# A conditioned transformer block in split float16 on one core: early transfers, GpSimd's tiles, scale inverses and held GELU steps put in another order

## The chip, the core and the metric

The chip is a Trainium2. The kernel runs on one of its cores, which has a matrix engine (TensorE, PE in the profile), a vector engine (VectorE, DVE), an engine for functions of single elements (ScalarE, ACT), a general engine (GpSimd, POOL) and an engine that only issues transfers here (SyncE, SP). Each engine takes its instructions in the order in which they were written down. They wait for one another by semaphores. The metric is the time of one execution on the device, in microseconds (us).

## The reference

A block of width 512 works on 2048 rows. Six modulation rows come from a condition vector. Attention has 32 query heads, 8 key and value heads and a window of the last 512 keys. The feed-forward part has an inner width of 1792 and a GELU gate.

```python
mod = silu(c) @ w_mod                       # sa, ca, ga, sb, cb, gb: six rows of 512
h = layernorm(x) * (1 + ca) + sa
q = (h @ wq)                                # 2048 rows, 32 heads of 128
k, v = k_cache[..., -512:, :], v_cache[..., -512:, :]   # 8 heads, each used by 4 query heads
p = softmax(q @ k.T * 128 ** -0.5)
x = x + ga * ((p @ v) @ wo)
h = layernorm(x) * (1 + cb) + sb
x = x + gb * ((gelu(h @ w_gate) * (h @ w_up)) @ w_down)  # gelu in its tanh form
```

All inputs and the output are float32.

## The kernel before

**Products.** Each product of two float32 matrices is three float16 matmuls: both operands are split into a high half, which is the rounded value, and a low half, which is the remainder, and high x high, low x high and high x low are added up (`mm3`, lines L86, L87 and L88). A half pair is made in one of two ways. `split_post` (L631 to L633) takes the high half on ScalarE and the low half on VectorE; it is used for queries (`qt`) and for attention outputs (`ot`). `halves` (L148 to L153) does both on GpSimd; it is used for weights, keys and values, after a multiplication by their scale (`times`, L156). The probabilities `p` are split in `high` (ScalarE, L883) and `low` (VectorE, L888).

**Scales.** So that float16 holds the values, each tile of weights, keys or values is multiplied by a scale that comes from its sum of squares. ScalarE sums the squares by partition (L212), TensorE adds over the partitions (`sums`, L216, the bank `pst`), VectorE copies the sum out (L177, L179 or L227), GpSimd raises it to the power one half and multiplies it on (L229, L233), and VectorE takes the reciprocal (`kinv` L244, `lr` L259, `wsc` L267, `osc` L280, `dsc` L303, `vsc` L606). The reciprocal is not written down at once: `then` (L235) puts it into the list of a later slot, two slots on. GpSimd's weight steps that use the scale come after it.

**Slots.** Attention is 512 slots. A slot t handles one tile of 128 query rows of one head: TensorE's scores `ps`, VectorE's maximum (L862), ScalarE's exponential (L871). In the same slot the probabilities of slot t - 2 get their high half and those of slot t - 3 their low half. `low` also issues the transfer that transposes `p` into `pt` (a DMA transpose on SP's queue), from which TensorE later forms `po`, probabilities times values. Between these steps TensorE takes three pieces of other work from a list: query products `pq`, `po`, and the output products `py`, which read the tiles `wo`. After that the slot runs its lists: plain steps (stores among them), the loads ("l") and the tile steps ("w"). What `then` and `split_post` put off runs in the list "d", ahead of the exponential.

**Groups.** 16 slots form a group, which starts at slot t0 = 16 g and uses one pair of query heads with its weight tiles `w`. There are two halves of 16 groups, one for each half of the rows. In the first half the tiles are made; most are stored (`kept`) and read back in the second half. The tiles of groups 1 and 2 are made by `plain_steps`. From group 3 on the weights are combined to sums and differences for a product with seven terms (`set_steps`, steps s0 to s4; their places before t0 stand in `SETPOS`, for group 3 in `SETPOS2`).

**Where the work is put.** A helper `sched` gets a list of slots for the steps of one tile. It puts the load some three slots ahead of the first step, as far as a free buffer allows (five buffers `raw`, two buffers `rw`). Other things are put at a slot by hand with `at`: the stores of the first keys and values, the loads and steps of the differences of input blocks (`sched_combos`; `CB` is their base slot), and the steps of `wo`. The four tiles of `wo` for a pair of groups are read twice: `WOS` lists the slots for the sums of squares and `WOP` those in which GpSimd multiplies them by `gs` (gate row times scale, L551) and splits them. One row of these tables is for the first pair of groups, one for the second, and so on; a fourth row of `WOP` serves the pairs 6 and 7. `k_items` and `v_items` do the same for keys and values. All transfers are issued on SP's one queue in the order written down, each waiting there until its buffer is free.

**The feed-forward part.** In the second half of attention, `prep_set` (weights of gate and up) and `prep_wd` (weights of down) make its tiles in the same manner. After slot 512 its products run. The first gate results are held back: `result` is put into the list `hold`, and in slot T + 2 = 514 the held tiles are worked off one after the other. Each goes through four steps: ScalarE squares (L1149), VectorE adds and multiplies, ScalarE takes tanh, VectorE multiplies (L1153). ScalarE's copy `fg<-fa` (L772) empties a bank that TensorE needs for its next product.

Of the kernel before, what the change touches and what calls it, by code (L numbers as in the profile page):

```python
# [17 lines left out]
P = 128  # L18
# [45 lines left out]
def block_kernel(ctx: ExitStack, tc: tile.TileContext, x, kT, v, wq, wo, wg, wu, wd, cT, wc, wm, out):  # L64
# [170 lines left out]
    def then(fn):  # L235

        if now[0] < 0:
            fn()
        else:
            at(("d", now[0] + 2), fn)  # L240

    def k_spread(g, m, go=True, ps=None):
        norm2(col("kmax", g), m, 1, 1.0, ps)
        inv = lambda: nc.vector.reciprocal(col("kinv", g), col("kmax", g))  # L244
        return then(inv) if go else inv
# [6 lines left out]
    def w_spread(pr, m, w=None):  # L252
# [13 lines left out]
        if now[0] >= 0:  # L266
            then(lambda: (nc.vector.reciprocal(col("wsc", pr), w), inv(), last()))  # L267
# [324 lines left out]
    def v_items(g):  # L592
# [7 lines left out]
        def spread():  # L600
# [5 lines left out]
            then(lambda: nc.vector.reciprocal(col("vsc", g), w))  # L606
# [408 lines left out]
    at(7, lambda: store(("k", 0), KV[0, 0, 0]))  # L1015
    at(9, lambda: store(("v", 0), KV[0, 0, 1]))
# [66 lines left out]
    for g in range(NG):  # L1083
# [54 lines left out]
    def f_items(q, hold=None):  # L1138
# [6 lines left out]

        def result(key, src):
            if m == 0:
                sq = pool.tile([P, QB], F32, tag="v16", name="sq", bufs=2)
                nc.scalar.activation(sq, src, AF.Square, scale=col("finv", f_scale(q)))  # L1149
                nc.vector.scalar_tensor_tensor(sq, sq, 1.0 / GELU_A, src, op0=ALU.add, op1=ALU.mult)  # L1150
                nc.scalar.activation(sq, sq, AF.Tanh, scale=col("tsc", f_scale(q)))
                dst = tmp("fg") if key == "21" else src
                nc.vector.scalar_tensor_tensor(dst, sq, 1.0, src, op0=ALU.add, op1=ALU.mult)  # L1153
                G[n, key] = dst
# [51 lines left out]
    def prep_set(q, b):  # L1206
# [24 lines left out]
        def s2():  # L1231
# [5 lines left out]
        sched(b, (lambda: set_load(key, srcs, 0), [lambda: pair_stat(key, m, 0), nop]), b + 8, kind="rw")  # L1237
        sched(b + 1, (lambda: set_load(key, srcs, 1), [lambda: pair_stat(key, m, 1), lambda: f_spread(f_scale(q), m["m"]), s2, nop]),
              b + 4, b + 8, b + 9, kind="rw")
        sched(b + 6, (outs[0][1], [s0, keep_it(0)]), b + 9)  # L1240
        sched(b + 7, (outs[3][1], [s1, keep_it(3)]), b + 10)
        sched(b + 8, (outs[1][1], [lambda: made(1, RAW[key][0]), keep_it(1)]), b + 11)
        sched(b + 9, (outs[2][1], [lambda: made(2, RAW[key][1]), keep_it(2)]), b + 12)
# [250 lines left out]
```

## Time and profile before

| what | value |
| --- | --- |
| time, median of 3 runs | 1792.94 us (1790.93 to 1799.85) |
| profiled execution, its own time | 1795.36 us |
| its span in the profile | 1793.1 us |
| TensorE busy | 1739.8 us, 97% |
| VectorE busy | 1446.9 us, 81% |
| ScalarE busy | 1210.5 us, 68% |
| GpSimd busy | 873.6 us, 49% |
| transfers | 330.76 MB, 184 GB/s on the mean |

The profile shows one execution. A row of a group gives line, engine, operation, output and inputs with partitions x elements, the count, busy time and the mean time of one in ns. A row of a timeline gives the start in us, the duration, the engine, the line and the tiles; in square brackets behind it is the time for which the engine stood idle before, and what ended that wait. A row of a table by stretches begins with the stretch in us; it then gives, in order, its length with TensorE's busy time, and the busy times of weight loads, VectorE, ScalarE and GpSimd with their numbers of instructions, then the granted TensorE clock as a share of full speed, the mean busy share of the 16 DMA engines and GB/s. A row of a transfer gives the issuing queue, the count and the median us from issue to landing.

### The profile page before, as it was taken

How to read it: one execution, taken by the hardware profiler on the slowest of the kernel's cores; microseconds unless marked ns; L12 is line 12 of the kernel's file. 1: busy time of each engine (PE TensorE's matmuls, PEld its weight loads, DVE VectorE, ACT ScalarE, POOL GpSimd, SP SyncE). 2: the span in 40 equal slices, each digit the busy share in tenths (PEclk: the TensorE clock that was granted, in tenths of full speed). 3: DMA queues.
4: the chain of work that ended last, by engine and by line, in shares of the span. 5: the costliest groups of instructions: out<-in, count | busy, mean ns of one | idle time of the engine just before them, and what ended most of it. 6: DMA issues, size and time to landing. Idle time of an engine off the chain costs nothing.

```text
span 1793.1 us, 26035 instructions
## 1 busy us (share of the span) xinstructions
PE 1739.8 (97%) x8094; PEld 795.6 (44%) x8094; DVE 1446.9 (81%) x2518; ACT 1210.5 (68%) x2811; POOL 873.6 (49%) x1100
## 2 busy tenths in 40 slices
PE   7989999999999999999999999999998999999999
PEld 4434444444444444444444444444443444444443
DVE  7778889888888888888888888888885758676676
ACT  5867787887877777677778787777774355344342
POOL 4689768686787873236475565555520024000000
PEclk9989999999999999999999999999999999999999
DMA  6989798999999888999999999999885633252221
GB/s 223 214 180 225 180 218 206 235 200 227 214 211 211 194 189 164 228 214 238 200 206 202 233 217 202 212 214 203 197 191 137 213 124 112 74 176 86 86 68 56
DMA packets 663850, 330.76 MB, mean 184 GB/s; under 512 B 553248, under 2 KB 576032, under 8 KB 663712
## 3 DMA queue, kind: packets, MB, share of 16 engines
q1 hardware_dynamic: 663424, 328.58, 78.5%
q8 instruction: 64, 1.05, 0.2%
q14 instruction: 74, 0.61, 0.1%
q10 hardware_dynamic: 288, 0.52, 0.1%
HBM read 134.88 MB, written 59.90 MB: 109 GB/s over the span
## 4 chain that ended last, share of the span: by engine, by line
PE 62%; DVE 13%; POOL 9%; ACT 7%; issue 5%; DMA 4%; SPq 0%; POOLq 0%; ACTq 0%; DVEq 0%
PE py L86 6%; PE py L87 6%; PE py L88 6%; PE ps L86 4%; PE ps L88 4%; PE ps L87 4%; PE po L86 3%; PE po L88 3%; PE po L87 3%; DVE p L888 3%; DVE nm L862 3%; PE fa L86 2%; PE fa L88 2%; PE fa L87 2%; ACT ee L871 2%
## 5 line engine op out<-in xcount | busy, mean ns | idle before, releaser
L871 ACT ACTIVATE ee<-ps,nm 128x512 f32<-128x512 f32 x512 | 350.9, 685 | 265.9 <-DVE nm L862 252.5
L888 DVE SCALAR_TENSOR_TENSOR p<-ee,rr,p 128x512 f16<-128x512 f32 x512 | 466.1, 910 | 0.0
L862 DVE TENSOR_REDUCE nm<-ps 128x1 f32<-128x512 f32 x512 | 349.2, 682 | 80.5 <-PE ps L88 78.6
L883 ACT ACTIVATE p<-ee,rr 128x512 f16<-128x512 f32 x512 | 365.2, 713 | 5.8 <-DMA pt<-p 5.2
L86 PE MATMUL ps<-k,qt 128*128 128x512 f16 x512 | 195.2, 381 | 18.2 <-DVE qt L633 12.4
L86 PE MATMUL po<-pt,v 128*128 128x512 f16 x512 | 195.3, 381 | 5.0 <-DMA pt<-p 2.4
L86 PE MATMUL py<-wo,ot 128*128 128x512 f16 x512 | 194.5, 380 | 1.8 <-DVE ot L633 1.8
L88 PE MATMUL po<-pt,v 128*128 128x512 f16 x512 | 195.3, 381 | 0.0
L87 PE MATMUL po<-pt,v 128*128 128x512 f16 x512 | 195.2, 381 | 0.0
L87 PE MATMUL ps<-k,qt 128*128 128x512 f16 x512 | 195.0, 381 | 0.0
L88 PE MATMUL ps<-k,qt 128*128 128x512 f16 x512 | 194.9, 381 | 0.0
L87 PE MATMUL py<-wo,ot 128*128 128x512 f16 x512 | 194.4, 380 | 0.0
L88 PE MATMUL py<-wo,ot 128*128 128x512 f16 x512 | 194.3, 379 | 0.0
L879 DVE RECIPROCAL rr<-rr 128x2 f32<-128x2 f32 x256 | 41.5, 162 | 98.7 <-ACT rr L876 96.6
L362 POOL TENSOR_TENSOR rs<-rs,nhalf 128x1 f32<-128x1 f32 x32 | 19.2, 600 | 195.4 <-DVE rs L356 192.8
L87 PEld LDWEIGHTS <-w 128*128 128x128 f16 x728 | 71.4, 98 | 93.4 <-issue 9.9
L88 PEld LDWEIGHTS <-w 128*128 128x128 f16 x728 | 71.5, 98 | 89.9 <-issue 5.3
L86 PEld LDWEIGHTS <-w 128*128 128x128 f16 x728 | 71.4, 98 | 89.4 <-POOL w L153 3.0
L839 DVE SCALAR_TENSOR_TENSOR acc<-py,dysc,acc 128x512 f32<-128x512 f32 x112 | 81.6, 746 | 30.5 <-PE py L88 29.6
L871 ACT ACTIVATION_READ_ACCUMULATOR ee<-ps,nm 128x1 f32 x512 | 100.5, 196 | 0.0
L839 DVE SCALAR_TENSOR_TENSOR acc<-py,ysc,acc 128x512 f32<-128x512 f32 x128 | 94.6, 739 | 3.3 <-PE py L88 3.3
L86 PEld LDWEIGHTS <-qt 128*128 128x128 f16 x512 | 50.5, 99 | 86.3 <-DVE qt L633 26.1
(253 smaller groups left out, 3850.5 us busy)
## 6 DMA issues: line engine op xcount, KB each, us to landing
w<-kept SPq DMA_DIRECT2D x123, 256.0 KB, 3.1
raw<-in_wo SPq DMA_DIRECT2D x64, 256.0 KB, 3.5
wo<-kept SPq DMA_DIRECT2D x60, 256.0 KB, 3.3
kept<-stage SPq DMA_DIRECT2D x56, 256.0 KB, 3.5
kept<-w SPq DMA_DIRECT2D x39, 256.0 KB, 3.1
rw<-in_wq SPq DMA_DIRECT2D x38, 256.0 KB, 3.5
hs<-hf SPq DMA_DIRECT2D x32, 256.0 KB, 2.7
pt<-p SPq DMA_TRANSPOSE x512, 3.5
```

Of the source, the lines that this page charges most:

```text
L86: nc.tensor.matmul(ps, llo, rhi, start=first, stop=False, skip_group_check=chain)
L87: nc.tensor.matmul(ps, lhi, rlo, start=False, stop=False, skip_group_check=chain)
L88: nc.tensor.matmul(ps, lhi, rhi, start=False, stop=last, skip_group_check=chain)
L362: nc.gpsimd.tensor_tensor(st["rs"], st["rs"], nhalf, op=ALU.pow)
L839: nc.vector.scalar_tensor_tensor(acc[ti], st["p"], by, acc[ti], op0=ALU.mult, op1=ALU.add)
L862: nc.vector.tensor_reduce(nm, E[t]["ps"], axis=AX.X, op=ALU.max, negate=True)
L871: nc.scalar.activation(e, E[t]["ps"], AF.Exp, bias=E[t]["nm"], scale=1.0, accum_out=sm[:, t % 2:t % 2 + 1])
L879: return lambda: nc.vector.reciprocal(r, r)
L883: nc.scalar.activation(p16[:, 0, :], E[t]["e"], AF.Copy, scale=E[t]["r"])
L888: nc.vector.scalar_tensor_tensor(p16[:, 1, :], E[t]["e"], E[t]["r"], p16[:, 0, :], op0=ALU.mult, op1=ALU.subtract)
```

## The change

Five places are edited. No arithmetic is added or taken away.

- The first 40 slots: the stores of the first keys and values go from slots 7 and 9 to 17 and 18. The sums of squares of the first four `wo` tiles, their splitting (`WOS`, `WOP`) and the loads for both go some two to three slots later; in the second pair of groups two of four splittings do, and pairs 6 and 7 get rows of their own. The weight tiles of group 2 are made in slots 19 and 21 (before 25 and 28), its key tile in 23 (before 27); the loads for them come earlier. Two loads and the first steps of the block differences go three to four slots later. The first steps of keys for some groups go one to two slots earlier or later, values are split one slot later and stored one later.
- The scale inverses: `then` puts the reciprocal three slots on instead of two. For the first groups it remains two.
- In accordance with that, step s0 of each weight set from group 3 on stands one slot later (`SETPOS`, `SETPOS2`).
- The weights of the feed-forward part: in `prep_set` and `prep_wd` the steps behind the inverse stand one slot later.
- The held GELU tiles: `hold` gets the four steps of a tile instead of one function. Two tiles at a time are worked off step by step: both squares, both inner steps, both tanhs, both outer steps. With three held tiles the third stays alone.

```diff
-WOS = ((12, 13, 15, 16), (-9, -8, -6, -5), (-16, -15, -14, -13))
-WOP = ((21, 22, 24, 26), (10, 12, 14, 16), (-6, -4, 10, 12), (-6, -4, -3, -2))
-SETPOS = (20, 15, 13, 12, 10, 8)
-SETPOS2 = (18, 13, 11, 10, 9, 7)
+WOS = ((15, 16, 17, 18), (-9, -8, -6, -5), (-16, -15, -14, -13))
+WOP = ((24, 26, 27, 28), (10, 12, 16, 17), (-6, -4, 10, 12), (-6, -4, 10, 12), (-6, -5, -3, -2))
+SETPOS = (20, 14, 13, 12, 10, 8)
+SETPOS2 = (18, 12, 11, 10, 9, 7)
...
-    def then(fn):
+    def then(fn, d=3):
 
         if now[0] < 0:
             fn()
         else:
-            at(("d", now[0] + 2), fn)
+            at(("d", now[0] + d), fn)
...
-        return then(inv) if go else inv
+        return then(inv, 3 if g > 1 else 2) if go else inv
...
-            then(lambda: (nc.vector.reciprocal(col("wsc", pr), w), inv(), last()))
+            then(lambda: (nc.vector.reciprocal(col("wsc", pr), w), inv(), last()), 3 if pr > 1 else 2)
...
-            then(lambda: nc.vector.reciprocal(col("vsc", g), w))
+            then(lambda: nc.vector.reciprocal(col("vsc", g), w), 3 if g else 2)
...
-    at(7, lambda: store(("k", 0), KV[0, 0, 0]))
-    at(9, lambda: store(("v", 0), KV[0, 0, 1]))
+    at(17, lambda: store(("k", 0), KV[0, 0, 0]))
+    at(18, lambda: store(("v", 0), KV[0, 0, 1]))
...
-                at(base + ((0, 0, 0, 2)[k] if p else (-10, -2, -1, -9)[k]), load)
+                at(base + ((0, 0, 0, 2)[k] if p else (-10, 2, 3, -9)[k]), load)
                 for off, fn in steps:
-                    at(("w", base + off), fn)
+                    at(("w", base + off + (3 if p == 0 and off < 7 else 0)), fn)
...
-            o = 1 if g > 1 else 2
-            sched_pair(g, srcs, t0 - 11 - o, spread, [(t0 - 6 - o, a)], [(t0 - (4 if g > 1 else 7), b)])
+            sched_pair(g, srcs, t0 - (19 if g > 1 else 13), spread, [(t0 - (13 if g > 1 else 8), a)], [(t0 - (11 if g > 1 else 7), b)])
...
-                    sched(t0 - (22 if g > 2 else 20), (load, [stat]))
-                    at(("w", t0 - (19 if g > 2 else 17)), spread_)
+                    sched(t0 - (22 if g > 2 else 18), (load, [stat]))
+                    at(("w", t0 - (19 if g > 2 else 16)), spread_)
                 load, stat, spread_, parts = k_items(pr)
-                sched(t0 - (7 if g > 2 else 5 if g > 1 else 6), (load, [parts]))
-                at(t0 - (3 if g > 2 else 1 if g > 1 else 2), lambda pr=pr: store(("k", pr), KV[0, pr, 0]))
+                sched(t0 - (7 if g > 2 else 9 if g > 1 else 6), (load, [parts]))
+                at(t0 - (3 if g > 2 else 5 if g > 1 else 2), lambda pr=pr: store(("k", pr), KV[0, pr, 0]))
                 if pr % 2 == 0:
                     load, stat, spread_, parts = v_items(qd)
-                    sched(t0 + 1, (load, [stat, spread_, parts]), t0 + 3, t0 + 5)
-                    at(t0 + 9, lambda qd=qd: store(("v", qd), KV[0, qd, 1]))
+                    sched(t0 + 1, (load, [stat, spread_, parts]), t0 + 3, t0 + 6)
+                    at(t0 + 10, lambda qd=qd: store(("v", qd), KV[0, qd, 1]))
             if pr % 2 == 0:
-                wo_items(qd, [t0 + o + (qd == 7) for o in WOS[min(qd, 2)]], [t0 + o for o in WOP[min(qd, 2) + qd // 6]])
+                wo_items(qd, [t0 + o + (qd == 7) for o in WOS[min(qd, 2)]], [t0 + o for o in WOP[min(qd, 2) + qd // 6 + qd // 7]])
...
+        def gelu(key, src):
+            b = {}
+
+            def square():
+                b["sq"] = pool.tile([P, QB], F32, tag="v16", name="sq", bufs=2)
+                nc.scalar.activation(b["sq"], src, AF.Square, scale=col("finv", f_scale(q)))
+
+            def inner():
+                nc.vector.scalar_tensor_tensor(b["sq"], b["sq"], 1.0 / GELU_A, src, op0=ALU.add, op1=ALU.mult)
+
+            def tanh():
+                nc.scalar.activation(b["sq"], b["sq"], AF.Tanh, scale=col("tsc", f_scale(q)))
+
+            def outer():
+                dst = tmp("fg") if key == "21" else src
+                nc.vector.scalar_tensor_tensor(dst, b["sq"], 1.0, src, op0=ALU.add, op1=ALU.mult)
+                G[n, key] = dst
+
+            return square, inner, tanh, outer
+
...
-                hold.append(lambda: result(key, src))
+                hold.append(gelu(key, src))
...
-        sched(b, (lambda: set_load(key, srcs, 0), [lambda: pair_stat(key, m, 0), nop]), b + 8, kind="rw")
+        sched(b, (lambda: set_load(key, srcs, 0), [lambda: pair_stat(key, m, 0), nop]), b + 9, kind="rw")
...
-        sched(b, (lambda: load(0), [lambda: stat(0), nop]), b + 6)
+        sched(b, (lambda: load(0), [lambda: stat(0), nop]), b + 7)
...
             if t == T + 2:
-                for fn in hold:
-                    fn()
+                for k in range(1, len(hold), 2):
+                    for step in zip(*hold[k:k + 2]):
+                        for fn in step:
+                            fn()
                 hold.clear()
```

More of the change, by code (lines that the diff above doesn't have):

```diff
@@ L1144, in add @@
             nc.vector.tensor_tensor(st[k], st[k], st[src], op=ALU.add)
+        def gelu(key, src):
[12 more added lines that the diff above has]
+            return square, inner, tanh, outer
         def result(key, src):
             if m == 0:
[L1148 to L1154, printed above, removed]
+                for step in gelu(key, src):
+                    step()
             else:
@@ L1235, in s2 @@
             tt(r0[:, r], r0[:, r], r0[:, l], ALU.subtract)
-        sched(b, (lambda: set_load(key, srcs, 0), [lambda: pair_stat(key, m, 0), nop]), b + 8, kind="rw")
+        sched(b, (lambda: set_load(key, srcs, 0), [lambda: pair_stat(key, m, 0), nop]), b + 9, kind="rw")
         sched(b + 1, (lambda: set_load(key, srcs, 1), [lambda: pair_stat(key, m, 1), lambda: f_spread(f_scale(q), m["m"]), s2, nop]),
[L1239 to L1243, printed above, removed]
+              b + 4, b + 9, b + 10, kind="rw")
+        sched(b + 7, (outs[0][1], [s0, keep_it(0)]), b + 10)
+        sched(b + 8, (outs[3][1], [s1, keep_it(3)]), b + 11)
+        sched(b + 9, (outs[1][1], [lambda: made(1, RAW[key][0]), keep_it(1)]), b + 12)
+        sched(b + 10, (outs[2][1], [lambda: made(2, RAW[key][1]), keep_it(2)]), b + 13)
     def prep_wd(n, b):
@@ L1267, in make @@
             halves(outs[k][0]["t"], st[k])
[L1269 to L1270 removed]
+        sched(b, (lambda: load(0), [lambda: stat(0), nop]), b + 7)
+        sched(b + 1, (lambda: load(1), [lambda: stat(1), spread, nop]), b + 4, b + 9)
         for k in range(2):
[L1272 removed]
+            sched(b + 7 + 2 * k, (outs[k][1], [lambda k=k: make(k), lambda k=k: store(("wd", n, k), outs[k][0]["t"])]), b + 10 + 2 * k)
     at(T // 2 + 34, lambda: mod_row(5))
```

2 lines of the change are left out of this document (removed).

## The prediction

> **What bounds the kernel now.** I read the page first: busy times and the 40 slices.
>
> ```profile
> span 1793.1 us, 26035 instructions
> PE 1739.8 (97%) x8094; PEld 795.6 (44%) x8094; DVE 1446.9 (81%) x2518; ACT 1210.5 (68%) x2811; POOL 873.6 (49%) x1100
> ...
> PE   7989999999999999999999999999998999999999
> ...
> PEclk9989999999999999999999999999999999999999
> ```
>
> TensorE is the bound. It is idle for 53 us of 1793, and only that idle time, and time at a reduced clock, can be won without removing work. The low digits lie at the start and near slice 31. So the next views were the busy times by stretch, for the clock, and TensorE's own timeline, for the gaps.
>
> ```profile
> 60.00:70.00 10.00, 7.61 (x28) 2.92 (x27) 6.50 (x12) 7.25 (x19) 3.92 (x4) 0.83 1.16 202
> 90.00:100.00 10.00, 5.25 (x22) 1.94 (x20) 9.29 (x15) 7.58 (x18) 9.34 (x13) 0.90 0.77 184
> 100.00:110.00 10.00, 7.89 (x23) 2.88 (x23) 4.12 (x8) 4.85 (x13) 9.43 (x10) 0.59 0.78 198
> 180.00:190.00 10.00, 10.00 (x40) 4.25 (x39) 6.56 (x11) 5.31 (x12) 7.47 (x12) 0.83 0.61 139
> 540.00:550.00 10.00, 9.04 (x35) 3.74 (x35) 8.79 (x17) 7.69 (x19) 9.24 (x14) 0.83 0.70 162
> ```
>
> The third number from the right is the granted clock. A clock of 0.83 over 10 us is 1.7 us of matmul time lost; 0.90 and 0.59 are 1.0 and 4.1. Each of these stretches holds or follows a gap of TensorE:
>
> ```profile
> 63.41 0.38 PE L86 MATMUL po<-pt,v 128*128 128x512 f16 x1 [2.37 <-issue]
> ...
> 86.02 0.39 PE L86 MATMUL ps<-k,qt 128*128 128x512 f16 x1 [0.68 <-DVE qt L633]
> ...
> 91.62 0.38 PE L86 MATMUL po<-pt,v 128*128 128x512 f16 x1 [1.54 <-DMA pt<-p]
> ...
> 98.88 0.61 PE L86 MATMUL ps<-k,qt 128*128 128x512 f16 x1 [3.21 <-DVE qt L633]
> ...
> 102.45 0.61 PE L86 MATMUL pq<-b,w 128*128 128x512 f16 x1 [2.11 <-POOL w L153]
> ...
> 141.01 0.39 PE L86 MATMUL po<-pt,v 128*128 128x512 f16 x1 [0.23 <-POOL v L153]
> ...
> 179.10 0.17 PE L216 MATMUL pst<-lm,ones 128*128 128x4 bf16 x1 [2.79 <-DVE qt L633]
> ...
> 540.96 0.39 PE L86 MATMUL ps<-k,qt 128*128 128x512 f16 x1 [1.69 <-DVE qt L633]
> ...
> 626.20 0.39 PE L86 MATMUL ps<-k,qt 128*128 128x512 f16 x1 [1.44 <-ACT p L883]
> ```
>
> Slot t begins where TensorE starts the scores (`ps`) of step t: 86.02 is slot 24, 98.88 slot 28, 179.12 slot 55. VectorE stands behind most gaps, and what it waited for in turn is GpSimd's scale chain (columns: start, duration, then idle before and its releaser):
>
> ```profile
> 94.15 0.17 DVE L259 RECIPROCAL lr<-lt 128x1 f32<-128x1 f32 x1 [0.71 <-POOL lt L233]
> ...
> 159.30 0.16 DVE L244 RECIPROCAL kinv<-kmax 128x1 f32<-128x1 f32 x1 [0.72 <-POOL kmax L233]
> ...
> 165.28 0.16 DVE L259 RECIPROCAL lr<-lt 128x1 f32<-128x1 f32 x1 [1.25 <-POOL lt L233]
> ...
> 536.52 0.17 DVE L267 RECIPROCAL wsc<-lw 128x1 f32<-128x1 f32 x1 [1.26 <-POOL lw L233]
> 537.95 0.16 DVE L259 RECIPROCAL lr<-lt 128x1 f32<-128x1 f32 x1 [1.26 <-POOL lt L233]
> ...
> 622.59 0.16 DVE L267 RECIPROCAL wsc<-lw 128x1 f32<-128x1 f32 x1 [1.85 <-POOL lw L233]
> ```
>
> **Part 1, loads and stores of slots 7 to 18.** Nothing is added or removed on SP's queue; DMAs change places. Before, four stood ahead of slot 10's transpose of p in slot 9 (store of v, `u<-hs`, `in_wo`, `in_kT`), two more behind it. After, slot 9 holds none; slots 10 to 15 hold 1, 2, 1, 2, 3, 1, and the stores of k and v go out in 17 and 18.
>
> ```profile
> pt<-p SPq DMA_TRANSPOSE x7, 4.8
> ```
> ```profile
> pt<-p SPq DMA_TRANSPOSE x512, 3.5
> ```
>
> The first row is the stretch from 50 to 70 us, the second the whole run, both in us to landing. The DMA engines were full (share 1.16 in 60 to 70), and the transpose that TensorE wanted for `po` at 63.41 landed behind the four. With them gone, gap and clock go: 2.37 + 1.7 = 4.1 us. Given back: the busier slots 13 to 15 delay the transposes of slots 11 to 14, which `po` of slot 17 reads. A transpose there lost 4.8 - 3.5 = 1.3 us on the mean; I charge 0.8. Value 3.3, ends 0 (the jam only moves) and 4.1. The wq loads now wait in slots 10 and 11 for GpSimd to have read group 1's tiles; those were read some 2 us before the slots' transposes go out, so SP does not stand.
>
> **Part 2, GpSimd's tiles of slots 19 to 32.** Group 2's weight tiles (once slots 25 and 28) and its k tile (27) are made in 19, 21 and 23; the four wo tiles go from 21, 22, 24, 26 to 24, 26, 27, 28. The same instructions, into time when GpSimd was idle:
>
> ```profile
> 71.28 0.57 POOL L229 TENSOR_TENSOR kmax<-kmax,half__86 128x1 f32<-128x1 f32 x1 [4.39 <-DVE kmax L177]
> ...
> 79.36 0.24 POOL L233 TENSOR_SCALAR ysc<-ysc 128x1 f32<-128x1 f32 x1 [5.38 <-DVE ysc L227]
> ...
> 82.61 0.70 POOL L233 TENSOR_SCALAR gs<-gate,osc 128x512 f32<-128x512 f32 x1
> ...
> 102.36 1.76 POOL L551 TENSOR_TENSOR raw<-raw,gs 128x512 f32<-128x512 f32 x1
> ...
> 104.92 1.15 POOL L153 TENSOR_TENSOR wo<-raw,wo 128x512 f16<-128x512 f32 x1
> ```
>
> The wait for `w` at 102.45 goes: 2.11. VectorE's `lw`, `wsc`, `lr` leave slots 23 to 25 with the 0.71 wait: 0.71 + 0.45 (three small instructions of 0.15 to 0.2) = 1.16 of the 5.43 us (0.68 + 1.54 + 3.21) that a late VectorE costs there; the rest I leave, since p, the block differences and the evictions stay. The clock lost 1.0 + 4.1 = 5.1 from 98 to 108; with one gap instead of a string I keep one 1.7 and win 3.4. Sum 2.11 + 1.16 + 3.4 = 6.7. Ends: 2.1 (the `w` wait alone) and 12.6 (7.5 of gaps and 5.1). What is late next is wo, whose last tile ran from 102.36 to 106.07: 3.7 us a tile. The first of them starts behind `gs`, at 82.61 before; three tiles of group 2, of some 3 us each, now stand ahead of it and fill the 5.38 us before 79.36, so I place it 4.0 later, at 86.6, and the fourth tile's end at 86.6 + 0.7 + 4 x 3.7 = 102.1. TensorE reads that in slot 31, about 103 by this sum: a cover of 1 us.
>
> **Part 3, v of slot 38.**
>
> ```profile
> 140.92 2.66 POOL L687 TENSOR_TENSOR rw<-rw 128x256 f32<-128x256 f32 x3
> ```
>
> These three steps of group 3 stood behind v and now stand ahead of it. `po` of slot 41 waited 0.23 for it at 141.01, so it had no cover. TensorE arrives 10 us earlier (3.3 + 6.7) and GpSimd about as much. I charge 0.8, ends 0 and 2.9.
>
> **Part 4, inverses three slots on.** VectorE's reciprocal stands one slot (2.6 us) later behind GpSimd's chain, and GpSimd's first weight step with it. The waits of 0.72 + 1.25 before slot 54 end, so of the 2.79 gap 0.8 is left and the clock stays: 2.0 + 1.7 = 3.7 (ends 0 and 4.5). At 541 two waits of 1.26 cover the 1.69 gap, and two of qd 6's wo tiles leave GpSimd's queue ahead of it: 1.69 + 1.7 = 3.4. At 626 (1.44) the wait of 1.85 is under a slot. Sum 4.8, I take 4.2; ends -2 (the queues are re-sorted over 300 slots, and a new gap like that of 541, without its clock, is possible) and 4.8.
>
> **Part 5, GELU by pairs.** Two of the held tiles are interleaved; the third stays alone.
>
> ```profile
> 1370.54 0.69 ACT L1149 ACTIVATE sq<-fa,finv 128x512 f32<-128x512 f32 x1 [0.89 <-DVE fg L1153]
> ...
> 1375.56 0.58 ACT L772 ACTIVATE fg<-fa 128x512 f32<-128x512 f32 x1
> ```
> ```profile
> 1376.19 0.38 PE L86 MATMUL fa<-t,w 128*128 128x512 f16 x1 [2.59 <-ACT fg L772]
> ...
> 1378.87 0.38 PE L86 MATMUL fa<-t,w 128*128 128x512 f16 x1 [1.22 <-ACT fg L772]
> ```
>
> The copy `fg<-fa` that TensorE waits for stood behind the squares and tanhs in turn. The second square now runs with the first, and the copy stands ahead of the third tanh: about 2 us earlier, after which it waits for TensorE's own product. The last copy now stands behind the fourth tile's steps and gives back about 1. Value 1.2, ends -0.5 and 1.8.
>
> **Sum.** 3.3 + 6.7 - 0.8 + 3.7 + 4.2 + 1.2 = 18.3 off the profiled execution's 1795.36 us: 1777.1. That execution lies 2.4 us above the median, 1792.94. The ends together give 1798.7 and 1767.7.
>
> By the rows, gaps of 1.69 to 3.21 us are followed by half clock, that of 2.59 at 1376 is not (slice 31 shows 9). The Trainium skill, TensorE: Matmul & The Clock Gate, Part 1, says that the clock halves after an idle window of some 3.4 us. Read as a wholly idle window, none of these gaps would cost clock, and the sum without the 8.5 us of clock would be 1785.6; the rows decide for the longer sum, and the rule's windows could explain why 2.59 went free.
>
> **The rivals.**
> *VectorE becomes the bound in slots 17 to 28.* GpSimd's work comes to lie beside VectorE's split of p:
>
> ```profile
> L888 DVE SCALAR_TENSOR_TENSOR p<-ee,rr,p 128x512 f16<-128x512 f32 x10 | 8.7, 867 | 0.0
> ```
> ```profile
> L888 DVE SCALAR_TENSOR_TENSOR p<-ee,rr,p 128x512 f16<-128x512 f32 x7 | 7.2, 1033 | 0.0
> ```
>
> These are 62 to 82 us, GpSimd half idle, and 82 to 102, GpSimd full; the shortest is 0.73. At 0.3 us more in each of eight slots that is 2.4 us, and the strings of gaps with their clock (3.4 + 1.7) would stay: 1777.1 + 2.4 + 5.1 = 1784.6. Against it: VectorE still has room there, 6.50 us busy of the ten from 60. The Trainium skill, SBUF — State Buffer, "SBUF: two separate sides", has the mechanism: a GpSimd instruction and a VectorE one with two SBUF inputs exclude each other for an instruction's whole length. The longer L888 agrees.
>
> *The wait moves to wo or v.* If GpSimd runs 4 us later than I place it, slot 31 waits 3 us, the clock of part 2 (3.4) is not won, and v costs its 2.9: 1777.1 + 3 + 3.4 + 2.1 = 1785.6. For it: the cover is 1 us and the placing an estimate.
>
> *All the gaps go:* 1767.7.
>
> *Slower: the tile comes too late.* The first weight tile of each group 3 to 15 is made a slot later, and slot 54 reads group 4's:
>
> ```profile
> 171.59 1.16 POOL L153 TENSOR_TENSOR w<-rw,w 128x512 f16<-128x512 f32 x1
> ```
> ```profile
> 173.55 0.38 PE L86 MATMUL ps<-k,qt 128*128 128x512 f16 x1
> ```
>
> It was done at 172.75, 1.4 us before its use. Wherever GpSimd's queue leaves less than 2.6 us, TensorE waits the rest. From 18.3 us over 13 groups (1.4 each) on, the gain is eaten; a whole slot each is 33.8: 1810.9. Against it: this chain ran late behind wo tiles, and one of these now stands behind it.
>
> **How the numbers follow.** The forecast, 1770 to 1784 with its likeliest 1777, has 0.55; VectorE bound (1785) 0.12; the moved wait (1786) 0.14; all gaps 0.10; slower 0.09. No change means within 0.5% of 1792.94, 1784.0 to 1801.9, about what a measurement of this kernel can tell. Faster: 0.55 + 0.10 + a third of 0.12 and of 0.14, whose times lie at that bound = 0.73 (rounded down); same 0.18; slower 0.09. The range 1765 to 1793 reaches from all gaps gone, less the 2.4 us between the profiled execution and the median, to no gain at all; it leaves out the slower case and little else.
>
> **What would show it.** No gap near 61 us and none for `w` in slot 28; a granted clock near 1.0 where 0.59 stood; slot 32 at about 106 instead of 116; no VectorE wait for `lr` near slot 50 or at 530; `fg<-fa` waiting under 1 us. Wrong would be: `py` waiting for wo in slot 31, `po` for v in 41 by over 2 us, weight tiles waited for at the start of later groups, or SP standing for GpSimd in slots 24 and 25, with p's transposes behind it.

## The result and the profile after

The changed kernel is slower. Its median is 1802.97 us (1799.69 to 1805.99), that of the kernel before, run beside it, 1792.94 us (1787.77 to 1799.85): a ratio of 1.0055, with an interval from 1.0036 to 1.0073. My forecast was 1777, in a range from 1765 to 1793. The profiled execution of the changed kernel has a span of 1804.2 us, 11.1 more than the one of before.

From the page of the changed kernel, the busy times and two rows of the 40 slices:

```profile
span 1804.2 us, 26006 instructions
PE 1742.8 (97%) x8094; PEld 798.7 (44%) x8094; DVE 1442.0 (80%) x2518; ACT 1210.7 (67%) x2811; POOL 873.5 (48%) x1100
...
PE   6989999999999999999999999999998999999999
...
PEclk9999999999999999999999999999999999999999
```

The work is the same; TensorE's idle time has moved and grown. Where, is told by the starts of the scores `ps` of a few slots in both traces (us from the start of the span; the last column is worked out from the two before it):

| slot | before | after | after less before |
| --- | --- | --- | --- |
| 0 | 25.71 | 25.70 | 0.0 |
| 13 | 59.58 | 64.45 | 4.9 |
| 16 | 69.16 | 71.20 | 2.0 |
| 28 | 98.88 | 101.38 | 2.5 |
| 41 | 139.33 | 141.24 | 1.9 |
| 43 | 144.91 | 151.82 | 6.9 |
| 56 | 183.40 | 187.86 | 4.5 |
| 196 | 540.96 | 544.32 | 3.4 |
| 197 | 545.25 | 546.90 | 1.7 |
| 208 | 573.79 | 575.93 | 2.1 |
| 213 | 586.50 | 596.09 | 9.6 |
| end of the span | 1793.1 | 1804.2 | 11.1 |

So some of the gain that I forecast at slots 13, 55 and 196 is there (2.8, 2.4 and 1.7 us in these steps), but three losses stand against it: 4.9 us ahead of slot 13, 5.0 at slot 41 and 7.5 in slots 208 to 213. TensorE's own timeline of after names the waits:

```profile
71.20 0.39 PE L86 MATMUL ps<-k,qt 128*128 128x512 f16 x1 [1.41 <-DVE qt L633]
76.31 0.38 PE L86 MATMUL po<-pt,v 128*128 128x512 f16 x1 [1.00 <-DMA pt<-p]
...
101.38 0.39 PE L86 MATMUL ps<-k,qt 128*128 128x512 f16 x1 [1.39 <-ACT p L883]
108.94 0.58 PE L86 MATMUL po<-pt,v 128*128 128x512 f16 x1 [3.50 <-DMA pt<-p]
...
146.34 0.61 PE L86 MATMUL po<-pt,v 128*128 128x512 f16 x1 [3.65 <-POOL v L153]
...
583.42 0.38 PE L86 MATMUL ps<-k,qt 128*128 128x512 f16 x1 [1.56 <-ACT ee L871]
591.00 0.61 PE L86 MATMUL ps<-k,qt 128*128 128x512 f16 x1 [3.43 <-DVE qt L633]
...
1385.33 0.38 PE L86 MATMUL fa<-t,w 128*128 128x512 f16 x1 [2.05 <-ACT fg L772]
1387.47 0.38 PE L86 MATMUL fa<-t,w 128*128 128x512 f16 x1 [0.69 <-ACT fg L772]
1391.02 0.38 PE L86 MATMUL fa<-t,w 128*128 128x512 f16 x1 [2.10 <-ACT fu L772]
```

Answering to the gaps shown of before: those at 63.41 (`po`), 102.45 (`w`) and 540.96 (`qt`) have no counterpart. New are the late transpose at 108.94, a wait for v of 3.65 where there were 0.23, two gaps with their forerunners near 590, and one for `fu<-fa`. The clock, from the busy times by stretch of after (third number from the right), went with them:

```profile
100.00:110.00 10.00, 5.12 (x21) 2.16 (x22) 7.35 (x12) 7.67 (x19) 9.48 (x9) 0.93 0.79 187
140.00:150.00 10.00, 6.35 (x23) 2.40 (x22) 3.79 (x7) 3.91 (x10) 9.43 (x12) 0.83 0.94 229
540.00:550.00 10.00, 10.00 (x51) 4.84 (x50) 8.44 (x18) 8.17 (x21) 6.78 (x10) 1.00 0.84 136
590.00:600.00 10.00, 9.00 (x29) 3.58 (x30) 7.65 (x15) 7.21 (x20) 9.32 (x13) 0.66 0.59 130
```

Won: 1.00 at 540, where before had 0.83, and 0.93 from 100 on, where it had 0.59. Lost: 0.83 at 140 and 0.66 at 590, where before had 1.00. The row of before from 590 to 600:

```profile
590.00:600.00 10.00, 9.67 (x47) 4.31 (x46) 9.05 (x17) 7.13 (x17) 5.95 (x11) 1.00 0.93 172
```

### The profile page after: what moved, and what is told of

It is laid out like the page before. It is cut to its first block, busy times and chain, and to the rows that moved or that the text cites. A ratio compares the mean times of both kernels' runs of the same rounds, so it can differ in the third digit from the quotient of the medians.

```text
span 1804.2 us, 26006 instructions
## 1 busy us (share of the span) xinstructions
PE 1742.8 (97%) x8094; PEld 798.7 (44%) x8094; DVE 1442.0 (80%) x2518; ACT 1210.7 (67%) x2811; POOL 873.5 (48%) x1100
## 3 DMA queue, kind: packets, MB, share of 16 engines
q8 instruction: 64, 1.05, 0.2%
## 4 chain that ended last, share of the span: by engine, by line
PE 54%; DVE 20%; ACT 12%; POOL 5%; DMA 5%; issue 5%; SPq 0%; POOLq 0%; ACTq 0%; DVEq 0%
DVE p L888 6%; PE py L86 5%; PE py L88 5%; PE py L87 5%; DVE nm L862 4%; ACT ee L871 3%; PE ps L86 3%; ACT p L883 3%; PE ps L87 3%; PE ps L88 3%; PE po L86 3%; PE po L88 3%; PE po L87 3%; PE fa L86 2%; PE fa L88 2%
## 5 line engine op out<-in xcount | busy, mean ns | idle before, releaser
L888 DVE SCALAR_TENSOR_TENSOR p<-ee,rr,p 128x512 f16<-128x512 f32 x512 | 460.3, 899 | 0.4 <-ACT p L883 0.2
L86 PE MATMUL po<-pt,v 128*128 128x512 f16 x512 | 195.0, 381 | 11.6 <-DMA pt<-p 7.2
```

The source lines that it names most:

```text
L86: nc.tensor.matmul(ps, llo, rhi, start=first, stop=False, skip_group_check=chain)
L888: nc.vector.scalar_tensor_tensor(p16[:, 1, :], E[t]["e"], E[t]["r"], p16[:, 0, :], op0=ALU.mult, op1=ALU.subtract)
```

## The experiments

All ratios are to the kernel before, run beside each. Some of them are a second step on another experiment; then two ratios are compared, each uncertain by 0.11 to 0.19%, so that a difference of less than some 0.2% tells nothing by itself. For scale: 0.1% is 1.8 us.

| kernel | what it is | median, us | ratio | interval |
| --- | --- | --- | --- | --- |
| after | the change | 1802.97 | 1.0055 | 1.0036 to 1.0073 |
| e1_early | before, only the order of the first 40 slots | 1794.49 | 0.9991 | 0.9976 to 1.0005 |
| e2_inverse | before, only the inverses and what moves with them | 1796.37 | 1.0003 | 0.9991 to 1.0016 |
| e3_gelu | before, only the GELU pairs | 1796.78 | 1.0016 | 1.0000 to 1.0031 |
| e4_wo6 | after, pair 6's wo tiles undone | 1798.24 | 1.0022 | 1.0010 to 1.0034 |
| e5_wo6_v | e4, group 3 and v of slot 38 undone | 1790.76 | 0.9974 | 0.9963 to 0.9985 |
| e6_wo6_v_gelu | e5, GELU pairs undone | 1791.01 | 0.9980 | 0.9967 to 0.9993 |
| e7_cb | e6, block differences undone | 1787.16 | 0.9955 | 0.9940 to 0.9970 |
| e8_inverse_v | e2, group 3 and v undone | 1790.75 | 0.9976 | 0.9964 to 0.9988 |
| e9_stores | e7, stores of k and v undone | 1789.86 | 0.9969 | 0.9957 to 0.9982 |
| e10_wo3 | after, one load a slot later | 1805.07 | 1.0054 | 1.0035 to 1.0072 |
| e11_g2 | e7, group 1's and 2's tiles undone | 1796.75 | 1.0005 | 0.9988 to 1.0023 |
| e12_best | e7 with e10's load | 1786.99 | 0.9953 | 0.9935 to 0.9971 |

### Pair 6's wo tiles and the block differences (e4_wo6)

The place to start was the greatest new loss. In after, slots 202 and 204 split two wo tiles that before had split ahead of the group. Slots 201 to 208 also hold the block differences of the next rows (`cb`). Four rows of after's timelines of GpSimd, ScalarE and VectorE, in order of time:

```profile
576.27 1.28 POOL L551 TENSOR_TENSOR raw<-raw,gs 128x512 f32<-128x512 f32 x1 [1.28 <-DMA raw<-in_wo]
...
580.68 1.27 POOL L476 TENSOR_TENSOR cb<-cb 128x512 f32<-128x512 f32 x1
...
581.98 0.63 ACT L339 ACTIVATE t<-cb 128x512 f16<-128x512 f32 x1 [2.27 <-POOL cb L476]
...
582.74 0.17 DVE L879 RECIPROCAL rr<-rr 128x2 f32<-128x2 f32 x1 [3.91 <-ACT rr L876]
```

A wo tile waits for its load and stands ahead of `cb` on GpSimd; ScalarE takes its instructions in order, waits for `cb` and comes late to `rr`; VectorE waits for `rr`, and TensorE for the scores' other steps and for `qt`. The test:

```diff
-WOP = (..., (-6, -4, 10, 12), (-6, -4, 10, 12), (-6, -5, -3, -2))
+WOP = (..., (-6, -4, 10, 12), (-6, -4, -3, -2), (-6, -5, -3, -2))
```

> The changed kernel with the splitting of pair 6's last two wo tiles back in its old slots (ahead of group 12, as before, and not 10 and 12 slots into it). Theory: these two tiles and their loads meet the block differences of slots 201 to 208 on GpSimd and on SP's queue, so that ScalarE waits for cb and rr comes late: the 7.9 us of slots 208 to 213 go, and some of the gap near 541 us (1.69, with clock) comes back: 4 to 8 us less than after, 1795 to 1799. Rival (the later inverses do it): within 2 us of after, 1801 to 1805, with the gaps of slots 208 to 213 still there.

Measured: 1.0022 against 1.0055, 0.33% or 6.0 us. In TensorE's timeline of e4 the stretch of slots 208 to 213 keeps one gap over half a microsecond:

```profile
584.69 0.39 PE L86 MATMUL ps<-k,qt 128*128 128x512 f16 x1 [0.55 <-DVE qt L633]
```

The theory holds, within the forecast numbers. The gap near 541 came back only as 0.45 us and without its clock, so the move of wo was not needed for that gain.

### Group 3's steps and v of slot 38 (e2_inverse, e8_inverse_v, e5_wo6_v)

Before, three of four L687 steps of group 3 stood behind v on GpSimd. After, all four stand ahead of it, and s0 and s1 in front of them end later:

```profile
135.02 1.47 POOL L153 TENSOR_TENSOR w<-rw,w 128x512 f16<-128x512 f32 x1
...
139.45 3.80 POOL L687 TENSOR_TENSOR rw<-rw 128x256 f32<-128x256 f32 x4
...
145.14 1.15 POOL L153 TENSOR_TENSOR v<-raw,v 128x512 f16<-128x512 f32 x1
```

e2_inverse takes the inverses alone to the kernel before; e8_inverse_v and e5_wo6_v then undo the part that touches slots 36 to 38. The core of the edit, as made on e4 (on e2 the line of `wsc` has `pr > 2`):

```diff
-SETPOS2 = (18, 12, 11, 10, 9, 7)
+SETPOS2 = (18, 13, 11, 10, 9, 7)
...
-            then(..., 3 if pr > 1 else 2)                # wsc, lr
+            then(..., 3 if pr > 3 else 2)
-            then(..., 3 if g else 2)                     # vsc
+            then(..., 3 if g > 1 else 2)
-                    sched(t0 + 1, (load, [stat, spread_, parts]), t0 + 3, t0 + 6)
+                    sched(t0 + 1, (load, [stat, spread_, parts]), t0 + 3, t0 + (6 if qd > 1 else 5))
```

(In e2 the first scale of wo and the scales of group 2 keep two slots, since there the old slots of their steps would come too early.)

> The kernel before with only the inverses three slots on, the weight steps behind them, the feed-forward weights' steps and v's split moved with them (the first wo scale and group 2's keep two slots). Theory: the gaps at slot 54 (2.79) and 541 us (1.69) shrink or go with their 3.4 us of clock, three gaps of 0.7 us for pst (slots 119, 151, 182) come in, v of slot 38 comes late as in after, 2 to 5 us: in all -4 to +2 us, 1789 to 1795, and no string of gaps in slots 208 to 213. Rival: the later inverses are what starves slots 208 to 213 (7.9 us there in after); then 1796 to 1802 with that string. My forecast's parts 3 and 4: 3.4 us faster, 1789.5.

> As e2 (inverses three slots on, all else as before), with group 3's inverse, its s0 and the second pair's v in their old slots. Theory: e2's loss of 5.1 us at slot 41 goes and its gains at slot 54 (4.0 us) and 541 us (3.4) stay: 5 us below e2, ratio about 0.9975. Rival: the gains of e2 are draws of one trace, and the runs show no more than 1 to 2 us, 0.999 to 1.000.

> The changed kernel with pair 6's two wo tiles back (as in e4) and, besides, group 3's inverse, its step s0 and the second pair's v (slots 36 to 38) back in their old slots. Theory: v of slot 38 was late in after, in e2 and in e4 alike because group 3's steps, a slot later, stand ahead of it; 5.0 us of e4's trace at slot 41 go: ratio to before 0.9994 where e4 had 1.0022. Rival: GpSimd as a whole runs late there, and v stays late by 2 us or more: ratio about 1.001.

Measured: 1.0003, 0.9976 and 0.9974; the first two as the theory had it, the third with a larger gain than its 0.9994. The wait is in e2, in the otherwise old order, and gone to the level of before in e8 (one row of TensorE's timeline from each):

```profile
142.87 0.39 PE L86 MATMUL po<-pt,v 128*128 128x512 f16 x1 [3.68 <-POOL v L153]
```

```profile
143.40 0.39 PE L86 MATMUL po<-pt,v 128*128 128x512 f16 x1 [0.59 <-POOL v L153]
```

Undoing it is worth 0.27% (4.8 us) in the order of before and 0.48% (8.6 us) on e4; the traces show 5.1 us at slot 41, with the clock. On e4 the same edit also goes with the gap at slot 54: 2.13 us in e4, 0.68 in e5. e2's string of gaps at 208 to 213 is absent, so the inverses do not cause it.

### The first 40 slots (e1_early, e7_cb, e11_g2, e9_stores, e10_wo3, e12_best)

My parts 1 and 2 together held 10.0 us. e1_early is the kernel before with nothing else changed:

```diff
-WOS = ((12, 13, 15, 16), ...)
-WOP = ((21, 22, 24, 26), ...)
+WOS = ((15, 16, 17, 18), ...)
+WOP = ((24, 26, 27, 28), ...)
... (and, as in the change: the stores in 17 and 18, sched_combos, sched_pair and k_items)
```

> The kernel before with only the new order of the first 40 slots (stores of k and v, the first wo tiles, group 2's tiles, the block differences); inverses, v's split, the later wo rows and GELU as before. Theory: the trace of after gains 4.2 us in slots 13 and 14 and 2.9 in slots 28 and 29, and loses 3.9 in slots 16 to 24 and, because SP stands in slot 25 for a raw buffer that GpSimd still reads, 3.5 ahead of po near 109 us; the 6.8 us at half clock ahead of slot 13 are a draw of that one execution. Then this kernel lies within 0.3% of before (1788 to 1798), with an SP stand of 3 us or more in slot 25 and a gap of TensorE over 2 us behind it. Rival: the moved transfers cost the clock at the start; then 1797 to 1802 and a stretch of 10 us at half clock ahead of slot 13 in this trace too. My forecast's parts 1 and 2: 10 us faster, 1783.

Measured: 0.9991, a gain of 1.6 us with an interval from a gain of 4.3 to a loss of 0.9. SP stands 2.9 and 2.1 us in that trace and the gap of `po` behind it is 2.14, near what was expected. The theory's range held; the forecast of 10 us is excluded. The sign that the rival named is in this trace too: slot 13 starts at 64.51, as in after. The rival's time of 1797 to 1802 did not come; what the clock ahead of slot 13 depends on is taken up below.

Why so little? One reason is in GpSimd's timeline of after:

```profile
74.34 1.27 POOL L476 TENSOR_TENSOR s<-u,s 128x512 f32<-128x512 f32 x1 [12.27 <-DMA u<-hs]
...
97.06 1.71 POOL L153 TENSOR_TENSOR k<-raw,k 128x512 f16<-128x512 f32 x1
...
99.44 0.69 POOL L233 TENSOR_SCALAR gs<-gate,osc 128x512 f32<-128x512 f32 x1
```

GpSimd is idle for 12.27 us, since the load of `u` now comes in slot 13, and everything that the change meant for slots 17 to 28 queues up behind it. `gs` came at 99.44, the fourth wo tile ended at 115.31; my sum had 86.6 and 102.1. Of the 12.8 us between the two times of `gs`, 4.9 are the late start of slot 13. Counted from slot 13, `gs` came after 35.0 us in after and 34.7 in e10, where my sum had 27.0. e7_cb puts only the block differences back (on top of e6, which is e5 without GELU pairs):

```diff
-                at(base + (... else (-10, 2, 3, -9)[k]), load)
+                at(base + (... else (-10, -2, -1, -9)[k]), load)
-                    at(("w", base + off + (3 if p == 0 and off < 7 else 0)), fn)
+                    at(("w", base + off), fn)
```

> As e6, with the first block differences (their loads and GpSimd's steps) back in their old slots, three earlier. Theory: in after GpSimd stood idle for 12.3 us up to 74 us, waiting for the load of u, and then had no gap until 119 us; what lay behind came late, so that SP stood 3.5 us in slot 25 and gs came at 99.4 where my sum had 86.6. With the differences early, GpSimd starts on them near 62 us, SP does not stand in slot 25, and TensorE's gaps in slots 16 to 29 shrink by 3 to 6 us: ratio about 0.996. Rival: their loads in slot 9 bring back the late transpose that po of slot 13 waited for (2.4 us with clock 4.1), and nothing is won: 0.998 to 1.000.

Measured: 0.9955 against 0.9980, 0.25% or 4.5 us. From slot 13 to slot 41 e7's trace is 3.7 us shorter than e6's. In e7's timeline GpSimd starts on them without idling, and `gs` comes 3.5 us earlier than in e6, where it stood at 97.32 (2.2 earlier, counted from slot 13):

```profile
61.39 1.27 POOL L476 TENSOR_TENSOR s<-u,s 128x512 f32<-128x512 f32 x1
...
93.84 0.69 POOL L233 TENSOR_SCALAR gs<-gate,osc 128x512 f32<-128x512 f32 x1
```

One detail was forecast wrong: SP still stands 3.2 us in slot 25, without a gap of `po` behind it.

e11_g2 and e9_stores take two other pieces out of e7:

```diff
-            sched_pair(g, srcs, t0 - (19 if g > 1 else 13), spread, [...], [...])     # e11: and the old slots of k_items
+            o = 1 if g > 1 else 2
+            sched_pair(g, srcs, t0 - 11 - o, spread, [(t0 - 6 - o, a)], [(t0 - (4 if g > 1 else 7), b)])
...
-    at(17, lambda: store(("k", 0), KV[0, 0, 0]))                                       # e9
-    at(18, lambda: store(("v", 0), KV[0, 0, 1]))
+    at(7, lambda: store(("k", 0), KV[0, 0, 0]))
+    at(9, lambda: store(("v", 0), KV[0, 0, 1]))
```

> e7 with group 1's and 2's weight tiles and keys back in their old slots (group 2's in 25, 28 and 27). Theory, my forecast's part 2: the wait for w in slot 28 (2.1 us) comes back, with qt late in front of it, and some of the clock: 4 to 6 us above e7, ratio 0.998 to 0.999. Rival: with the wo tiles moved behind, GpSimd has room for group 2 in the old slots: within 1 us of e7.

> e7 with the stores of the first k and v back in slots 7 and 9. My forecast's part 1 held four transfers of slot 9 responsible for the late transpose at 63 us; in e7 the block differences' loads are back in slot 9, without that gap. Theory: the stores, with the wo loads that also left these slots, are what mattered: the gap of po in slot 13, 1.2 to 2.4 us in the traces with the old order, comes back and with it 1 to 3 us: ratio 0.9965 to 0.997 against e7's 0.9955. Rival: the wo loads alone did it, and e9 equals e7.

Measured: 1.0005 and 0.9969 against e7's 0.9955: 0.50% (9.0 us) and 0.14% (2.5 us). Group 2's early tiles are the change's best piece, worth more than I or the theory gave (from slot 13 to slot 41 e11's trace is 8 us longer than e7's). They are so in this order, in which the wo tiles stand late; without them TensorE waits for `w` and then for wo, which is split behind it (e11's timeline):

```profile
99.40 0.61 PE L86 MATMUL pq<-b,w 128*128 128x512 f16 x1 [4.60 <-POOL w L153]
...
114.58 0.38 PE L86 MATMUL py<-wo,ot 128*128 128x512 f16 x1 [3.10 <-POOL wo L152]
```

For the stores the size is as expected, but not the place. e9's trace has no gap of `po` near 61 us, although the store of v and the load of `u` are back in slot 9. Its wait for `qt` at 69.71 is 2.88 us, where e7 has 2.40. Behind SP's stand it has a gap of `po` of 2.18 us at 105.59, which e7 has not, but e5 and e6 have one there too (2.35 and 4.59) with the stores in their new slots. Whether the stores cost anything is open: 0.14% lies inside the uncertainty.

SP's stand in slot 25 is a row of its own in the waits of after (queue and line, releaser: us, times, longest):

```profile
SPq L533 <- POOL wo L153: 3.5, 1, 3.5
```

A load for the fourth wo tile waits for a buffer that GpSimd still reads, with p's transpose behind it on the queue, and `po` at 108.94 is 3.50 late. e10_wo3 issues that load behind the transpose:

```diff
-WOP = ((24, 26, 27, 28), ...
+WOP = ((24, 26, 27, 29), ...
```

> The changed kernel, except that the load for the fourth wo tile of the first pair is issued one slot later (26), behind the next transpose of p; its splitting is given slot 29, and the order of GpSimd's instructions is the same as in after. Theory: SP's stand of 3.56 us in slot 25, behind which p's transpose and po of slot 28 waited 3.50, goes or falls under 1 us: 3 to 4 us less than after's 1.0055, ratio 1.0035. Rival: TensorE waits for VectorE in that stretch anyway (e7's trace has SP's stand of 3.29 and no gap of po behind it), and the ratio stays within 0.1% of 1.0055.

Measured: 1.0054, nothing won; but each ratio is uncertain by 0.19%, and the 0.20% of the theory lies within that, so that the traces have to decide. SP still stands 2.2 us, where under 1 was expected. The gap of `po` is gone, and in its place TensorE's timeline of e10 has waits for the wo tiles themselves:

```profile
104.44 0.38 PE L86 MATMUL py<-wo,ot 128*128 128x512 f16 x1 [0.33 <-POOL wo L152]
105.68 0.38 PE L87 MATMUL py<-wo,ot 128*128 128x512 f16 x1 [0.86 <-POOL wo L153]
108.06 0.38 PE L86 MATMUL py<-wo,ot 128*128 128x512 f16 x1 [1.79 <-POOL wo L152]
109.29 0.38 PE L87 MATMUL py<-wo,ot 128*128 128x512 f16 x1 [0.86 <-POOL wo L153]
```


These are 3.84 us for the 3.50 that went. From slot 13 to slot 41 e10 gains 3.2 us on before's trace and after 3.0. The rival holds in its verdict, but not in its reason: the stand was a real wait, and a wait of the same length for GpSimd's wo lay behind it.

e12_best is e7 with this load, and the fastest kernel here together with e7:

> e7 with the fourth wo load one slot later as in e10. Theory: SP does not stand in slot 25, but e7 had no gap behind that stand, so 0 to 1.5 us less than e7: ratio 0.9945 to 0.9955. Rival: the load, now nearer its use, makes wo late for slot 32: 1 to 2 us more.

Measured: 0.9953, not to be told from e7's 0.9955. Its gap in slot 31 (`py` for `ot` and wo) is 1.79 + 0.72 us where e7 has 0.95.

One more loss in these slots has ScalarE behind it. The stretch from slot 14 to slot 20, first of before, then of after:

```profile
65.50:77.40 11.90, 11.60 (x52) 4.97 (x50) 9.46 (x19) 9.87 (x27) 3.83 (x5) 0.93 1.00 192
```

```profile
67.04:81.41 14.37, 10.91 (x52) 4.49 (x50) 10.49 (x21) 13.99 (x37) 5.83 (x9) 1.00 1.10 248
```

ScalarE is busy for 13.99 of 14.37 us in after, for 9.87 of 11.90 in before: the sums of squares of group 2's weights and of the wo tiles now meet there. The stretch takes 11.6 to 12.3 us in the four traces with the old early order, 12.8 in e11, whose group 2 is in its old slots, and 14.3 to 15.9 in the nine others. No run moves the squares alone, so this cost of some 2.5 us is read from traces and not shown by an experiment.

### The held GELU tiles (e3_gelu, e5_wo6_v, e6_wo6_v_gelu)

e3 has only the `gelu` steps and the loop over pairs; e6 undoes them on e5.

```diff
-                for fn in hold:
-                    fn()
+                for k in range(1, len(hold), 2):
+                    for step in zip(*hold[k:k + 2]):
+                        for fn in step:
+                            fn()
```

> The kernel before with only the held GELU tiles worked off by pairs. Theory from the trace of after, which lost 2.3 us from slot 512's end to the third feed-forward product: 0 to +2.5 us, 1793 to 1795.5, with a wait of TensorE for fu<-fa of some 2 us that before does not have, and the wait for fg<-fa at 1376 shorter than 2.59. Rival, my forecast's part 5: 1.2 us faster, with no new wait.

> As e5, with the held GELU tiles one after the other again. Theory: the pairs cost what e3 showed, 0.16% or 2.9 us by the runs and 2.0 us by the traces: 2 to 3 us below e5, ratio about 0.998. Rival: e3's interval reached down to no effect; then within 1 us of e5.

Measured: 1.0016 for e3 (1.0000 to 1.0031), as the theory had it; but e6 has 0.9980 against e5's 0.9974, 0.06% the other way, which is the rival's number. The two together don't tell the pairs from no effect. In all traces with pairs the two waits for `fg` are 2.05 and 0.69 us (before: 2.59 and 1.22), and `fu` is waited for 2.10, which no trace without pairs has: 1.0 us lost against before. (In the traces without pairs the first of these waits is 2.44 to 3.30 us.) The clock behind these gaps scatters by more than that. e6, one after the other like before, has a gap of 2.60 where before had 2.59 (e6's gap and the stretch around it, then the stretch of before):

```profile
1371.74 0.38 PE L86 MATMUL fa<-t,w 128*128 128x512 f16 x1 [2.60 <-ACT fg L772]
```

```profile
1370.00:1380.00 10.00, 7.48 (x21) 2.67 (x21) 6.30 (x10) 5.06 (x9) 0.00 (x0) 0.66 0.00 0
```

```profile
1370.00:1380.00 10.00, 6.19 (x29) 2.67 (x28) 5.30 (x9) 5.45 (x9) 0.00 (x0) 1.00 0.08 26
```

The clock is 0.66 in e6; before, from 1370 to 1390, it was 1.00. From the product behind this gap to the first `py` TensorE took 7.73 us in e6 (1371.74 to 1379.47) and 5.45 in before (1376.19 to 1381.64). So the low clock cost 2.3 us. The 3.4 that 0.34 x 10 gives is too much, since TensorE was idle anyway for part of the time at low clock.

### The clock at the start

What is left are the 4.9 us ahead of slot 13, where the two orders hardly differ. The stretch from 25 to 60 us of five kernels, in the order before, after, e2_inverse, e8_inverse_v, e10_wo3:

```profile
25.00:60.00 35.00, 29.65 (x152) 15.83 (x153) 27.69 (x56) 24.26 (x57) 22.27 (x30) 0.95 0.69 174
```

```profile
25.00:60.00 35.00, 29.61 (x129) 16.93 (x130) 22.95 (x48) 20.69 (x48) 19.35 (x29) 0.80 0.54 136
```

```profile
25.00:60.00 35.00, 29.43 (x152) 16.15 (x153) 27.45 (x56) 24.25 (x57) 21.73 (x30) 0.95 0.70 172
```

```profile
25.00:60.00 35.00, 29.56 (x128) 16.84 (x129) 22.92 (x49) 20.75 (x48) 19.25 (x28) 0.80 0.55 143
```

```profile
25.00:60.00 35.00, 29.38 (x158) 15.90 (x159) 28.62 (x59) 24.51 (x57) 22.09 (x30) 1.00 0.67 155
```

e2 and e8 have the instructions of before up to slot 25 and beyond, and show 0.95 and 0.80; e10 has those of after, and shows 1.00 where after shows 0.80. e1, with the early order of after, shows 0.80, and e4, e5 and e6, with that order too, 0.90. So nothing ties the 0.15 x 35 = 5.3 us between before and after in this stretch to the change; both orders show high and low values. What draws it was not tried.

## Why the prediction was wrong

I forecast 18.3 us faster; it is 10 us slower. The step that failed first is the placing of GpSimd's early tiles (`gs` and wo); besides, one cost was put at nothing and one was far too small. In the order of its steps:

- **Part 1 (3.3 us) and part 2 (6.7 us): wrong in size, together.** e1 gives both 1.6 us, at most 4.3. The pieces are there: the gap at 63 and the wait for `w` went, the 0.8 charged for `po` of slot 17 measured 1.00, and group 2's early tiles alone are worth 9.0 us beside the old differences. The step that failed is the placing of `gs`. I moved it by GpSimd's own queue (three tiles ahead, 4.0 us later) and left out that the sums of squares, which it hangs on, move by two to three slots, and that the block differences' loads and steps move by three to four. That left GpSimd idle for 12.3 us up to 74.34, and the differences then took the room that I counted for group 2. `gs` came 12.8 us later than my 86.6, 8.0 of them behind slot 13. ScalarE has no term in my sum at all, and the sums of squares filled it from slot 14 to slot 20. My list of what would show it wrong had SP standing in slots 24 and 25; it stood 3.5 us in 25, and p's transposes with it.
- **The cover of wo (1 us) only seemed to hold:** in after TensorE waits in slot 31 only for `ot`, 0.75 us, because the stand of SP had held it up first. That is luck and no merit of the sum: e10 took the stand's gap away, and wo was late by 3.84. This was my rival of the moved wait, near its place and size; I gave it 0.14.
- **Part 3 (0.8 us lost, at most 2.9): too small.** I counted only the steps that change places with v. Its own split, a slot later, and s0 of group 3 ahead of it count too: a gap of 3.65 us and, at 0.83 for 10 us, up to 1.7 of clock. The runs give 4.8 to 8.6.
- **Part 4 (3.7 + 4.2 = 7.9 us): right in mechanism and place, half as large in the end.** e8 shows 0.24%, 4.3 us (2.2 to 6.5). In its trace slot 54 gains 3.8 and 541 gains 3.4, as I had it, and the gap of 1.44 at 626 is gone. But 3.4 of my 7.9 were clock: with the old inverses e3 lost none of it and e1 lost it at slot 54 alone. Between slots 57 and 195 e8 takes 1.3 us more than before, with two new gaps of 0.67 for `pst` in slots 118 and 150.
- **Not a term of my sum at all: pair 6's wo.** I saw that two of its tiles leave GpSimd's queue ahead of 541, and took that as help. Where they arrive, slots 202 and 204, I did not look; the block differences are there, and it costs 6.0 us. With part 3 this was the largest error after the early slots, and e4 shows it.
- **Part 5 (1.2 us): the sign is open.** The waits for `fg` became shorter by 0.54 and 0.53 us, not 2, and the third tile alone now delays `fu` by 2.10. The runs can't tell it from nothing.
- **VectorE as the bound:** its size came, its reason did not. Slots 16 to 24 take 19.3 us in after and 16.9 in before, the 2.4 that this rival named, and TensorE waits there for VectorE's `qt` (1.41, 1.05 and 1.16). But VectorE itself stood idle for 2.7 us from slot 16 to slot 20, 1.85 of them for `rr` from the full ScalarE; and in e7, with group 2's tiles just as early beside the split of p, these slots take 17.4. VectorE's long waits near 580 were for `rr` too, that is for ScalarE behind GpSimd.
- **The clock.** I priced each gap with the 3.4 us windows at half clock that before's trace had there. e6 lost 2.3 us behind a gap of 2.60 that cost before nothing, and the start lost 1.8 to 7 us with one order. Of the 8.5 us of clock in my sum, 5.1 were draws of one execution: the low clock behind slot 13 is in none of e2, e3 and e8, that at 541 in neither e1 nor e3, that at slot 54 in e1 and not in e3. The 3.4 of part 2 came: from slot 24 to slot 33, (1 - clock) times the length, which is the most that the clock can have cost, is 5.2 us in before, 3.4 to 3.5 in e2, e3 and e8, and 1.8 in after. The Trainium skill, TensorE: Matmul & The Clock Gate, Part 1, says that the window which decides is free-running and the result differs from run to run. The rows agree with that. The same part of the Trainium skill puts the low clock behind at least one idle window of some 3.4 us. If that means a wholly idle window, the rows contradict it, since no gap in e6's stretch is longer than 2.60.
- **The high end:** my parts add up to 27.8 us there, which gives 1767.6 and not 1767.7.

In sum, by the runs: the early order gains 1.6, the inverses 4.3; v gives back 4.8 to 8.6 and pair 6's wo 6.0; GELU, by its two values, is between 1 gained and 3 lost. These pieces come to 4 to 12 us slower, around the 10 measured; each of them is uncertain by some 2 us. Within the early order, the block differences' delay costs 4.5 us of what group 2's tiles and the stores bring.

## What to carry to other kernels

A tile step that is taken out of a crowded place has to be looked up in the place where it arrives: what is queued there on its engine and on the load queue, and which in-order engine waits behind it. When several steps of one chain move, place the last of them by the chain (load, sum, scale, tile), not by the engine's queue alone; one load moved later can turn the room you count on into idle time. Look also at every engine of the chain: the squares of the moved tiles filled ScalarE, which no term of the sum held. And what one trace shows of the clock behind a single gap may be a draw: price gaps, and put clock losses in the range.

## What the runs showed of the hardware

TensorE's clock over the same instructions from 25 to 60 us was 0.95 in before and e2 and 0.80 in e8; slot 13 began at 59.58, 59.65 and 64.56 us, a difference of 5 us in 1793. A gap of 2.59 to 2.60 us at the same place was followed by a clock of 1.00 in one execution (before) and of 0.66 over 10 us in another (e6), which cost 2.3 us. The 3.50 us for which TensorE waited behind a stand of the transfer queue went in e10, and the ratio stayed at 1.0054 (after: 1.0055, each uncertain by 0.19%), with 3.84 us of another wait in its place.
